# Another set of unread matmuls ahead of the first attention scores

## The chip, the core and the metric

The kernel runs on one core of one Trainium2 chip. Its engines are TensorE (PE; the loading of its weights is listed apart as PEld), VectorE (DVE), ScalarE (ACT), GpSimd (POOL) and SyncE (SP). The metric is the device time of one launch in microseconds, and the time of a kernel is the median of its runs. Profiles come from one execution of the program; its span runs from the first instruction to the last.

## The reference

Sliding-window causal attention (8 batches, 8 heads, 576 positions, head width 64, window 64) feeds a mixer block with a low-rank mix over positions and a two-layer MLP:

```python
scores = scale * q @ k.T                      # kept where 0 <= i - j < 64
attn   = softmax(scores) @ v                  # -> x: 8 x 576 x 512
h      = (x.T @ U) @ V                        # rank 32 over the 576 positions
u      = x + h.T
out    = u + relu(u @ w_ch1) @ w_ch2          # 512 -> 2048 -> 512
```

Inputs and output are float32. The kernel computes with bfloat16 operands and sums in float32.

## The kernel before, in words

Work is ordered by hand: the instructions of each engine stand in its queue in the order in which the Python code calls for them, and an engine takes them strictly in turn, waiting on semaphores for what they read. Loads are issued by POOL (lines 105, 126, 130, 197, 200 and so on).

The program has a prelude for batch 0 and then a loop over nine chunks of 512 rows of the flattened 4608 x 512 activations. A chunk's MLP has 16 column blocks of the first layer (`ch1`, matmuls at line 622, ReLU on ACT at line 633 or DVE at line 631) and then the second layer (`ch2`, line 664). Into the slots between these pieces the attention of the next batch is placed.

The prelude is where the change lies. In PE's queue it has, in this order:

- 91 matmuls called *unread*: `turn_over(91, P)`, line 721, with a 128 x 128 block of the zeroed tile `idle` as weights and 128 columns of the same tile as the moving operand. They write a PSUM tile that nothing reads. They wait only for the memset of `idle` (line 142).
- the scores of batch 0, groups S[0] and S[1] (matmuls at line 311), which need the transposed k and q. These are made on DVE at line 239: k and q of heads 0 to 3 first, then k and q of heads 4 to 7, each after its load.
- two more unread matmuls, of 512 columns: `turn_over(2)`.
- S[2] to S[5], each opened by two matmuls that add a bias (line 287), with the product with v (PV, line 398) between them. Exponentials are on ACT (line 322), masks on DVE (line 329).
- the transposes of the result through PE (line 518), the low-rank mix (lines 444 and 532), ten more unread matmuls of 128 columns, and then chunk 0.

`turn_over` is this helper; each matmul it issues is preceded in PE's queue by a load of its weights:

```python
def turn_over(n, cols=CH, to=None):
    for _ in range(n):
        nc.tensor.matmul(
            (unread if to is None else to)[:, 0, 0:cols],
            idle[:, 0:P],
            idle[:, 0:cols],
            start=to is None,
            stop=to is None,
        )
```

P is 128, W is 64, CH is 512.

Of the kernel before, what the change touches and what calls it, by code (L numbers as in the profile page):

```python
# [16 lines left out]
def kernel(  # L17
# [16 lines left out]
    P = nc.NUM_PARTITIONS  # L34
    W = 64
# [683 lines left out]
# [10 lines that stand above are left out]
    def fresh():  # L729
        return ps_big.tile([P, 2, CH], FP32, name="unread", tag="big")  # L730

    unread = fresh()
    turn_over(91, P)
    att = {0: attention(0, alone=True)}
    a = att[0]
    for f in a["KT"]:
# [125 lines left out]
```

## Time and profile before

| | |
|---|---|
| median of 6 runs | 322.24 us (320.11 to 323.67) |
| the profiled execution's own time | 323.67 us |
| its span | 322.0 us |
| busy in the span: PE / DVE / ACT / POOL | 313.9 / 209.4 / 106.2 / 104.3 us |
| mean granted TensorE clock | 0.979 |
| the 91 unread matmuls | 1.26 to 8.09 us, 219 ns median for one from issue to its modelled end |
| first scores on PE | from 8.29 us |

The busy time of a row counts a matmul from its start to its modelled end, and matmuls overlap; how often one starts is read from counts over a stretch. An idle time in brackets is followed by what ended it. The profile was taken in one execution, and the runs differ among themselves, so a sum is made against 323.67 and 322.0, and only then related to the median. In tables of stretches each engine has its busy time and, in brackets, the number of its instructions that touch the stretch; then come the clock, the share of the DMA engines and GB/s.

### The profile page before, as it was taken

How to read it: one execution, taken by the hardware profiler on the slowest of the kernel's cores; microseconds unless marked ns; L12 is line 12 of the kernel's file. 1: busy time of each engine (PE TensorE's matmuls, PEld its weight loads, DVE VectorE, ACT ScalarE, POOL GpSimd, SP SyncE). 2: the span in 40 equal slices, each digit the busy share in tenths (PEclk: the TensorE clock that was granted, in tenths of full speed). 3: DMA queues.
4: the chain of work that ended last, by engine and by line, in shares of the span. 5: the costliest groups of instructions: out<-in, count | busy, mean ns of one | idle time of the engine just before them, and what ended most of it. 6: DMA issues, size and time to landing. Idle time of an engine off the chain costs nothing.

```text
span 322.0 us, 7022 instructions
## 1 busy us (share of the span) xinstructions
PE 313.9 (97%) x2893; PEld 154.0 (48%) x2893; DVE 209.4 (65%) x368; ACT 106.2 (33%) x174; POOL 104.3 (32%) x156
## 2 busy tenths in 40 slices
PE   8799999999999999999999999999999999999995
PEld 8454454555444544454445444444444444444444
DVE  7543868679698759777957795769577722412211
ACT  1444353274206520552056203630273004203400
POOL 8681429430039403750384037502000200030000
PEclk9759999999999999999999999999999999999999
DMA  7999999999749994899999929993500150050011
GB/s 122 160 199 207 207 157 163 160 204 126 22 114 178 168 105 95 152 168 136 110 180 186 108 52 181 194 139 29 172 2 2 34 164 0 0 163 35 2 65 67
DMA packets 108930, 38.05 MB, mean 118 GB/s; under 512 B 98353, under 2 KB 101809, under 8 KB 108897
## 3 DMA queue, kind: packets, MB, share of 16 engines
q0 software_dynamic: 92480, 25.63, 111.4%
q1 hardware_dynamic: 11232, 10.69, 9.9%
q10 hardware_dynamic: 5184, 1.28, 1.8%
q8 instruction: 23, 0.38, 0.5%
q14 instruction: 11, 0.08, 0.1%
HBM read 48.94 MB, written 9.44 MB: 181 GB/s over the span
## 4 chain that ended last, share of the span: by engine, by line
PE 77%; DMA 12%; DVE 5%; POOL 2%; issue 2%; SPq 1%; ACT 1%; DVEq 0%; POOLq 0%
PE psA L622 32%; PE psU L664 31%; DMA qr<-in_q_dram 7%; DMA vA<-in_v_dram 4%; PE xr L398 3%; PE sc L361 3%; PE psv L473 2%; DVE un L484 1%; DVE stg L560 1%; PE psU L646 1%; SPq L586 1%; POOL kr L114 1%; PE sc L311 1%; PE xT L532 1%; PE xT L518 1%
## 5 line engine op out<-in xcount | busy, mean ns | idle before, releaser
L622 PE MATMUL psA<-uTc,w1b 128*128 128x512 bf16 x576 | 132.9, 380 | 0.0
L664 PE MATMUL psU<-w2b,c 128*128 128x512 bf16 x560 | 127.2, 379 | 0.0
L633 ACT ACTIVATE c<-psA 128x512 bf16<-128x512 f32 x101 | 60.3, 597 | 170.1 <-PE psA L622 170.1
L664 PEld LDWEIGHTS <-c 128*128 128x128 bf16 x560 | 53.5, 98 | 64.5 <-issue 1.9
L622 PEld LDWEIGHTS <-w1b 128*128 128x128 bf16 x576 | 53.4, 98 | 61.3 <-issue 0.2
L586 POOL DMA_DIRECT2D uTc<-stg x35 | 19.1, 556 | 117.1 <-DVE stg L560 77.8
L673 DVE TENSOR_TENSOR osb<-psU,un 128x512 f32<-128x512 f32 x35 | 23.5, 670 | 32.3 <-PE psU L664 32.2
L631 DVE TENSOR_SCALAR c<-psA 128x512 bf16<-128x512 f32 x43 | 29.5, 687 | 22.1 <-PE psA L622 20.5
L126 POOL DMA_DIRECT2D vA<-in_v_dram x32 | 28.2, 886 | 28.2 <-PE psA L622 9.9
L376 DVE TENSOR_TENSOR pts<-pts,mask 128x768 bf16<-128x768 bf16 x42 | 23.0, 556 | 19.8 <-ACT pts L369 17.4
L369 ACT ACTIVATE pts<-sc 128x768 bf16<-128x768 f32 x42 | 31.7, 811 | 3.7 <-PE sc L361 3.7
L484 DVE TENSOR_TENSOR un<-psv,xs 128x512 bf16<-128x512 f32 (+1 forms) x40 | 25.9, 674 | 9.8 <-PE psv L473 9.6
L417 DVE TENSOR_TENSOR xs<-xr,rcp 128x512 bf16<-128x512 f32 (+1 forms) x39 | 26.9, 691 | 1.3
L560 DVE STREAM_TRANSPOSE stg<-un 128x512 bf16<-128x512 bf16 x28 | 18.4, 683 | 0.0
L398 PEld LDWEIGHTS <-pts 128*64 128x64 bf16 x576 | 13.2, 116 | 10.7 <-DVE xs L417 4.7
L247 DVE STREAM_TRANSPOSE qt<-qr 128x576 bf16<-128x576 bf16 x20 | 15.8, 788 | 3.0 <-DMA vA<-in_v_dram 3.0
L114 POOL DMA_DIRECT2D qr<-in_q_dram x20 | 17.0, 851 | 2.1 <-DMA vA<-in_v_dram 1.8
L114 POOL DMA_DIRECT2D kr<-in_k_dram x20 | 16.9, 844 | 2.3 <-DMA vA<-in_v_dram 1.3
L247 DVE STREAM_TRANSPOSE kt<-kr 128x576 bf16<-128x576 bf16 x20 | 15.7, 787 | 1.9 <-DMA kr<-in_k_dram 1.9
L398 PE MATMUL xr<-vB,pts 128*64 128x65 bf16 x320 | 16.2, 202 | 0.6 <-PE xr L398 0.6
L361 PEld LDWEIGHTS <-kt 64*64 64x64 bf16 (+1 forms) x720 | 10.1, 106 | 9.3 <-issue 8.3
L361 PE MATMUL sc<-qt,kt 64*64 64x128 bf16 (+4 forms) x720 | 13.1, 215 | 0.2 <-DVE qt L239 0.2
(70 smaller groups left out, 165.7 us busy)
## 6 DMA issues: line engine op xcount, KB each, us to landing
out_dram<-osb SPq DMA_DIRECT2D x35, 256.0 KB, 2.3
kr<-in_k_dram POOLq DMA_DIRECT2D x26, 288.0 KB, 10.5
qr<-in_q_dram POOLq DMA_DIRECT2D x26, 288.0 KB, 12.1
vA<-in_v_dram POOLq DMA_DIRECT2D x32, 128.0 KB, 13.6
w2b<-in_moe_w_ch_dram POOLq DMA_DIRECT2D x2, 1024.0 KB, 18.3
uTc<-stg SPq DMA_DIRECT2D x42, 32.0 KB, 2.4
uTc<-stg ACTq DMA_DIRECT2D x35, 32.0 KB, 2.3
uTc<-stg POOLq DMA_DIRECT2D x35, 32.0 KB, 2.1
```

The lines of the kernel that those rows point to most:

```text
L114: nc.gpsimd.dma_start(out=dst[32 * part : 32 * (part + 1), off : off + NJJ * RD].rearrange("p (n x) -> p n x", x=r * D), in_=src[b, m * NJ ...
L126: nc.gpsimd.dma_start(out=va[:, t, :, 0:D], in_=v[b, :, t * P : (t + 1) * P, :].rearrange("h p d -> p h d"),)
L247: nc.vector.transpose(out=dst[:, n * S : (n + 1) * S].rearrange("q (m p e) -> q m e p", p=32, e=r), in_=src[:, 32 + n * RD : 32 + (n + 1) ...
L361: nc.tensor.matmul(sc[half * W : (half + 1) * W, g, (a - lo) * W : (z - lo) * W], operand("k", g, jj, e, kb * W, (kb + 1) * W), operand("q ...
L369: nc.scalar.activation(out=dst, in_=sc[:, :, 0 : PB * W].rearrange("p g (n w) -> p g n w", w=W), func=ACT.Exp, scale=scale,)
L398: nc.tensor.matmul(xr[r0 : r0 + W, h // 4, (h % 4) * VW : (h % 4 + 1) * VW], pts[:, g, jj * NB + blk, :], rhs, start=True, stop=True,)
L417: nc.vector.tensor_tensor(out=x[lo:hi, t, :, :].rearrange("p (a h) d -> p a h d", a=2), in0=xv[:, :, :, 0:D], in1=rcp[lo:hi].to_broadcast( ...
L484: nc.vector.tensor_tensor(out=u_tiles[g][rs, :], in0=ps[rs, n, :], in1=xt[n][rs], op=ALU.add)
L622: nc.tensor.matmul(to if c < 2 else to.rearrange("p (t i q) -> p t i q", i=4, t=TPC), w1b[:, dc, n * P : (n + 1) * P], uT_cols(dc), start= ...
L631: nc.vector.tensor_relu(out=c1[i][:], in_=ps)
L633: nc.scalar.activation(out=c1[i][:], in_=ps, func=ACT.Relu)
L664: nc.tensor.matmul(acc[t][:], c1[i][:, t * P : (t + 1) * P], w2b[:, i, :], start=(i == 0), stop=(i == NFC - 1),)
```

## The change

One call becomes two. The 91 matmuls of 128 columns give way to 70 of 64 columns, followed by 30 of 232 columns: 100 matmuls in place of 91, with 11,440 columns in place of 11,648. The weights of each are the same 128 x 128 block as before, loaded anew each time. The PSUM tile, its place in the pool and everything after it are unchanged, and no other engine's queue is touched.

```diff
     unread = fresh()
-    turn_over(91, P)
+    turn_over(70, W)
+    turn_over(30, 232)
     att = {0: attention(0, alone=True)}
```

## The prediction

> **What bounds the kernel now.** I read four views, from the whole to the place of the change. First the page's slices: TensorE (PE) is busy in nine tenths or more of nearly every fortieth of the span, so time taken out of PE's path shows in the end, and time put beside it doesn't.
>
> ```profile
> PE   8799999999999999999999999999999999999995
> PEclk9759999999999999999999999999999999999999
> ```
>
> The reader is to see that only the first three digits, some 24 us, fall short, both in work and in granted clock. The change lies in the first of them. Second, the order of time there:
>
> ```profile
> 1.26 6.83 PE L721 MATMUL unread<-idle 128*128 128x128 bf16 x91 [1.26 <-DVE idle L142]
> ...
> 5.90 1.25 DVE L239 STREAM_TRANSPOSE kt<-kr 128x576 uint32<-128x576 uint32 x1
> 7.00 1.24 DVE L239 STREAM_TRANSPOSE qt<-qr 128x576 uint32<-128x576 uint32 x1
> ...
> 8.29 0.76 PE L311 MATMUL sc<-qt,kt 32*64 32x128 bf16 x48 [0.19 <-DVE qt L239]
> ...
> 8.97 0.61 PE L721 MATMUL unread<-idle 128*128 128x512 bf16 x2
> ...
> 9.42 0.49 PE L287 MATMUL sc<-bias,ident 128*128 128x384 bf16 x2
> ...
> 10.15 1.26 DVE L239 STREAM_TRANSPOSE qt<-qr 128x576 uint32<-128x576 uint32 x1 [0.21 <-DMA qr<-in_q_dram]
> ...
> 11.47 0.85 PE L311 MATMUL sc<-qt,kt 32*64 32x128 bf16 x24 [1.56 <-DVE qt L239]
> ```
>
> The 91 unread matmuls end at 8.09. The first scores start at 8.29, and what lets them go is not PE but the transpose of q, which ends at 8.24. Later PE stands still again, for 1.56 us up to 11.47, for the second q transpose, and that one waits for its load. Third, the chain of waits says the same of what sets the end:
>
> ```profile
> 3.08 7.05 DMA qr<-in_q_dram
> 10.13 0.02 issue
> 10.15 1.27 DVE qt L239
> 11.42 0.04 issue
> 11.47 0.85 PE sc L311 x19
> ```
>
> No L721 of the first group stands in the chain: it runs from the q load through the transpose to the scores at 11.47, and from there mostly on PE. Fourth, the stretches, cut where the matmuls' rate or the granted clock changes:
>
> ```profile
> 1.26:4.60 3.34, 3.34 (x32) 3.34 (x33) 2.20 (x14) 0.84 (x1) 3.07 (x8) 1.00 0.57 89
> 4.60:8.03 3.43, 3.43 (x62) 3.33 (x60) 3.16 (x6) 0.00 (x0) 3.43 (x5) 1.00 1.11 200
> 8.03:11.43 3.40, 1.69 (x54) 1.15 (x53) 2.74 (x4) 1.51 (x2) 2.98 (x5) 1.00 1.97 166
> 11.43:14.84 3.41, 3.37 (x68) 1.78 (x71) 1.90 (x6) 1.62 (x2) 1.74 (x3) 0.50 2.22 145
> 14.84:18.26 3.42, 3.42 (x108) 2.49 (x102) 1.44 (x4) 1.52 (x2) 2.68 (x5) 0.50 1.45 191
> 21.67:25.08 3.41, 3.41 (x19) 2.06 (x19) 0.00 (x0) 0.96 (x2) 1.03 (x2) 0.50 1.14 213
> ```
>
> In brackets first stands the number of matmuls. 32 unread ones fit in the first stretch and 62 in the second of nearly equal length: 107 ns each, then 56 ns. So PE starts slow and is released at about 4.60 (the clock column reads 1.00 there although the rate says half; it is full only from 4.60). In 8.03:11.43 PE is busy for only 1.69 of 3.40 us, and from 11.43 to 25.08 the clock is 0.50. These 13.65 us at half clock, in which PE is nearly all of the chain, are the costly thing that the warm-up could touch.
>
> **The change, part by part.** *Removed:* 91 matmuls of 128 columns. 31 at 107 ns and 60 at 56 ns are 3.32 + 3.36 = 6.68 us, plus the last one's own tail, which gives the 6.83 of the row. *Added, seventy of 64 columns:* no row has 128-wide weights with 64 columns. From 128 columns in 107 ns slow, 64 take 53 ns if the columns set the pace. Until the release, 3.34 us after the start, 3.34 / 0.053 = 63 of them are done; the other 7 run at half of 56, 28 ns: 0.20 us. *Added, thirty of 232 columns:* 232/128 of 56 ns is 101 ns, thirty are 3.04 us. Sum: 3.34 + 0.20 + 3.04 = 6.58 against 6.68, so 0.1 us earlier: 11,440 columns in place of 11,648, and nine more instruction pairs that the columns cover. The last unread matmul ends at about 7.99. The cover is the transpose until 8.24: of the gain nothing is seen, and if the cover were gone it would be worth the 0.1 us.
>
> Is the pace of the short ones really set by columns? Each of them loads 128-wide weights anew. The row to go by is the attention product at half clock, whose weights also change every time:
>
> ```profile
> 17.42 1.40 PEld L398 LDWEIGHTS <-pts 128*64 128x64 bf16 x48
> ```
>
> 48 loads in 1.40 us, 29 ns for a load with its matmul of 65 columns, two of which (upper and lower half) go together. So a pair of instructions needs no more than 29 ns to issue, less than 53. The load itself: the Trainium skill, page "TensorE: Matmul & The Clock Gate", section "LDWEIGHTS (loading the stationary operand)", has a rule that speaks against the change: a load takes its number of columns over 1.2 ns, 107 ns for 128. By it the short ones would be bound by their loads: 31 until the release, 39 more at no less than 56 ns, 2.18 us, and the sum would be 3.34 + 2.18 + 3.04 = 8.56, PE free at 9.8. The rows are against it: the 62 matmuls of 4.60:8.03 each carry a 128-wide load and come every 56 ns, and a load over 128 columns (98 ns mean at full clock, L622) shows no longer than one over 64 (L361, 106). I take 53 ns, and keep 107 as the other end. Even then the 1.56 us of idle ahead of 11.47 plus the 0.19 ahead of 8.29 take up the delay of 1.7 us.
>
> What is queued behind on PE: the first two score groups, two unread matmuls of 512 columns, the first biases; for them wait the exponentials on ScalarE (8.87) and the masks on VectorE (11.26, behind the transposes until 11.41). A delay of up to about a microsecond is lost in that queue. DMA queues, SP, POOL, ScalarE and VectorE issue exactly what they did, in the same order.
>
> *The release itself.* Nothing in the rows shows how short matmuls count in whatever grants the clock. The same page, section "What's actually happening", says that the warm-up is some 3.4 us of time and not a number of matmuls; the trace's first release after 3.34 us agrees, and by that rule the release stays at 4.60: cost 0. But the stretch 14.84:18.26 is 3.42 of 3.42 us busy, mostly with matmuls of 64 and 65 columns, and the clock stays at 0.50 after it; 21.67:25.08, with 128 and 512 columns, is followed by full clock. The narrow weights there (32 rows, 64 columns) are one reading, the shortness another. So the other end: the seventy short ones don't count, 70 x 53 ns = 3.73 us are lost for the release, and only the thirty longer ones can earn it. Between these ends I take 0, because the short ones here use all 128 rows and columns.
>
> The span stays 322.0 and the profiled execution 323.67 (1.67 outside the span). That execution lies 1.43 above the median of 322.24; the edit touches nothing that makes this gap, so the forecast is carried over to the median: 322.2 us.
>
> **The rivals.** *Slower:* the short ones don't count, and the thirty don't earn the release in time. They run slow, 232/128 x 107 = 194 ns each: 3.73 + 5.82 = 9.55, PE free at 10.8. The two score groups at half clock (0.78 each, as from 11.47 to the biases), two unread of 512 at 427 ns and the biases (0.75) are 3.2 us: the scores of 11.47 start at 14.0 at the latest, about 2.3 us late with some overlap, and from there PE is the chain: 324.5. It decides once PE is free later than about 9.85. For it: the stretch of short matmuls that earned no clock. Against: there the array was partly used.
>
> *Faster:* PE is late but not too late (free at 9.5 to 9.9, by a release one stretch later, at 8.03, or by load-bound short ones). Then 8.03:11.43 has little idle time left, and the clock may not be taken at 11.43. One stretch of 3.41 us at full instead of half clock is worth up to 1.7 us: 320.5; two, with the exponentials (0.81 each) and value copies as new limits, perhaps 3: 319.2. For it: the clock fell right after the one stretch with PE half idle. Against: it needs the warm-up to be slower than its columns say, and the scores themselves, 32 rows deep, may not hold the clock.
>
> *No change because it isn't longer:* "nine more" is 2% fewer columns; that is the forecast itself.
>
> **How the numbers follow.** About 0.5% (1.6 us) is what a measurement of this kernel can tell from no change; the six runs alone go from 320.11 to 323.67. Forecast 0.47, with its own range 321.0 to 323.4; slower rival 0.31; faster rival 0.22. The range over the cases is 319.9 to 325.0: from between the two faster ends to a little past the slower one.
>
> **What would show it.** Right: seventy unread matmuls 53 ns apart until about 4.6 and thirty 100 ns apart, ending near 8.0; first scores still released by the q transpose; scores at 11.47 as before; half clock again for about four such stretches. The load rule is right if the short ones come 107 ns apart. The slower rival shows as thirty matmuls 194 ns apart and scores after 11.47 that wait for PE; the faster one as a clock above 0.50 between 11.4 and 14.8. The prediction is wrong above all if the release moves, or if the grid of these stretches lies elsewhere from one execution to the next and the two forms meet it differently.

## The result: 0.5% slower

The changed kernel takes 323.3 us in the median (30 runs) against 321.68 us of the kernel before (67 runs). The ratio is 1.0049, with a 95% interval of 1.0032 to 1.0065. The prediction was no change, 322.2 us. Executions more than 1.5% slower than the fastest of their kernel are left out of every ratio, mean and count.

The order of time of the changed kernel (start, length, engine, line, operation):

```profile
1.26 6.78 PE L721 MATMUL unread<-idle 128*128 128x64 bf16 x100 [1.26 <-DVE idle L142]
...
8.39 0.76 PE L311 MATMUL sc<-qt,kt 32*64 32x128 bf16 x48 [0.35 <-DVE qt L239]
...
12.13 1.25 DVE L239 STREAM_TRANSPOSE qt<-qr 128x576 uint32<-128x576 uint32 x1 [1.77 <-DMA qr<-in_q_dram]
12.65 0.54 POOL L206 DMA_DIRECT2D ub<-in_moe_U_dram  x1 [2.19 <-DMA qr<-in_q_dram]
13.44 0.85 PE L311 MATMUL sc<-qt,kt 32*64 32x128 bf16 x24 [3.43 <-DVE qt L239]
```

The first row merges both new sizes (100 matmuls). It ends at 8.04, a little earlier than before, and the first scores again wait for a transpose. The scores that stood at 11.47 now start at 13.44, and PE has idled for 3.43 us before them. The transpose of q is not to blame: it waited 1.77 us for its load. So did POOL, by 2.19 us, with the loads that it still had to issue. The chain of waits names the same load:

```profile
3.07 9.04 DMA qr<-in_q_dram
12.11 0.02 issue
12.13 1.27 DVE qt L239
13.40 0.04 issue
13.44 0.85 PE sc L311 x16
```

Before, this load stood there with 7.05 us and ended at 10.13. By the semaphore of the load, 15 of its 16 pieces had landed by 10.48 and the last one landed at 12.11; before, they landed by 9.78 and at 10.13. Two stretches of the DMA queues show what shared the way with it. From 8.5 to 10.1 us the changed kernel has this row; the kernel before has no row of that queue there, and has it from 10.1 to 11.2 (the second fence; the columns are packets, MB and share of 16 engines):

```profile
q8 instruction: 1, 0.02, 3.7%
```

```profile
q8 instruction: 1, 0.02, 5.4%
```

It is one packet of 16 KB, and it takes 0.94 us. That the queue brings PE's instructions is read from its count over the whole kernel: 23 packets here, 22 in a form below that has 90 PE instructions fewer. The packet starts at 9.86 us in the changed kernel, ahead of the last piece of q, and at 10.22 us before, just behind it (10.13). In this profile the last piece is 1.63 us behind the fifteenth, more than the packet's 0.94; what makes up the rest isn't shown. Last, the stretches of the changed kernel:

```profile
1.26:4.80 3.54, 3.54 (x67) 3.54 (x68) 2.24 (x15) 0.84 (x1) 3.28 (x9) 1.00 0.60 90
4.80:8.00 3.20, 3.20 (x38) 2.98 (x35) 3.10 (x6) 0.00 (x0) 3.20 (x4) 1.00 1.07 192
8.00:11.63 3.63, 1.66 (x53) 1.12 (x53) 1.59 (x2) 1.51 (x2) 2.46 (x4) 1.00 1.89 167
11.63:25.28 13.65, 11.10 (x212) 7.20 (x212) 7.05 (x17) 5.57 (x13) 9.40 (x14) 0.50 1.48 172
```

The release at 4.80 comes with 67 short matmuls in 3.54 us, 53 ns each. The half-clock time is 13.65 us again, in both profiled executions. One profile thus shows the late load. It can't show how often the clock falls. For that I counted stretches over all executions, since each run lists the mean granted clock.

### The profile page after: what moved, and what is told of

Its sections match the earlier page's. It is cut to its first block, busy times and chain, and to the rows that moved or that the text cites. A ratio compares the mean times of both kernels' runs of the same rounds, so it can differ in the third digit from the quotient of the medians.

```text
span 322.4 us, 7040 instructions
## 1 busy us (share of the span) xinstructions
PE 312.8 (97%) x2902; PEld 153.9 (48%) x2902; DVE 209.6 (65%) x368; ACT 106.2 (33%) x174; POOL 104.3 (32%) x156
## 4 chain that ended last, share of the span: by engine, by line
PE 64%; DMA 20%; DVE 6%; SPq 3%; issue 3%; POOL 3%; ACT 1%; POOLq 0%; DVEq 0%
PE psA L622 27%; PE psU L664 24%; DMA qr<-in_q_dram 10%; DMA vA<-in_v_dram 7%; SPq L586 3%; PE xr L398 3%; PE sc L361 2%; DMA uTc<-stg 2%; DMA kr<-in_k_dram 2%; PE psv L473 2%; POOL kr L114 1%; DVE stg L560 1%; PE psU L646 1%; PE sc L311 1%; DVE un L484 1%
## 5 line engine op out<-in xcount | busy, mean ns | idle before, releaser
L361 PE MATMUL sc<-qt,kt 64*64 64x128 bf16 (+3 forms) x720 | 13.1, 215 | 0.2 <-DVE qt L239 0.2
```

The lines of the kernel that those rows point to most:

```text
L361: nc.tensor.matmul(sc[half * W : (half + 1) * W, g, (a - lo) * W : (z - lo) * W], operand("k", g, jj, e, kb * W, (kb + 1) * W), operand("q ...
```

## The experiments

All forms were timed against the kernel before on the same chip, but for a third profile of the changed kernel, which is one execution. Only the prelude is edited. "Stretches" are half-clock stretches of 3.41 us: each takes 3.41 x 0.5 / 322 = 0.0053 off an execution's mean granted clock, so they can be counted from it. In 179 executions of the kernel before, 0, 1, 2, 3 and 4 stretches came 36, 44, 36, 27 and 36 times (1.91 on the mean), with medians of 320.98, 321.21, 321.48, 322.29 and 323.07 us. A line through these executions rises by 0.54 us for each stretch. The kernel before differs from set to set: beside the forms of the first theory it had 2.31 stretches on the mean, beside the later ones 1.63 to 1.75. In 31 executions of the changed kernel the counts were 0, 0, 4, 9 and 18.

The summary first. "144th" is when PE starts the 144th instruction of its queue (loads of weights and matmuls counted), "fetch" is the start of the first 16 KB packet of instructions, "q" is when the last piece of the second q load lands, all in us from one profile; stretches are means over the timed executions.

| kernel | 144th | fetch | q | stretches | ratio (95%) |
|---|---|---|---|---|---|
| before | 6.82 | 10.22 | 10.13 | 1.91 | 1 |
| changed: 70 x 64, 30 x 232 | 5.00 | 9.86 | 12.11 | 3.45 | 1.0049 (1.0032 to 1.0065) |
| the same again | 5.16 | 8.87 | 11.04 | 3.46 | 1.0056 (1.0033 to 1.0078) |
| the same, a third profile | 5.16 | 8.79 | 10.97 | | |
| 182 x 64 | 5.04 | 8.85 | 11.03 | 3.50 | 1.0067 (1.0027 to 1.0108) |
| 100 x 116 | 7.70 | 11.53 | 10.14 | 2.71 | 1.0004 (0.9981 to 1.0027) |
| 55 x 64, 36 x 225 | 6.48 | 10.23 | 10.05 | 1.67 | 0.9982 (0.9961 to 1.0004) |
| 46 x 254 | 9.14 | 12.75 | 10.19 | 2.29 | 0.9987 (0.9960 to 1.0014) |
| 109 x 107 | 6.98 | 11.39 | 10.12 | 1.58 | 1.0027 (1.0001 to 1.0053) |
| 30 x 232, 70 x 64 | 8.32 | 12.16 | 9.82 | 2.41 | 1.0017 (0.9996 to 1.0037) |
| before, q transposed late | 6.58 | 10.12 | 10.04 | 3.43 | 1.0050 (1.0027 to 1.0073) |
| before, filled | 7.78 | 11.50 | 10.02 | 0.76 | 0.9974 (0.9953 to 0.9995) |
| changed, filled | 5.16 | 8.85 | 11.03 | 0.64 | 1.0038 (1.0014 to 1.0061) |
| filled, q transposed late | 6.73 | 10.65 | 9.91 | 0.50 | 0.9997 (0.9976 to 1.0017) |

### First theory: more instructions bring the fetch forward

My first theory was that eighteen more instructions put the fetch in front of q. Its rival was that the short matmuls shift the clock's release. Four forms of the warm-up with nearly the same number of columns separate number and size.

```diff
-    turn_over(91, P)
+    turn_over(100, 116)
```

> 100 unread matmuls of 116 columns: as many instructions as the changed kernel, 11,600 columns, no short ones. Fetch theory (the block of PE's instructions, 16 KB, is fetched at 9.86 us instead of 10.22, because 18 more instructions stand ahead of it, and holds up the last piece of the second q load): slower than before like the changed kernel, ratio 1.004 to 1.006, the fetch at 9.6 to 10.0, q landed at about 12. Rival (the short matmuls shift the clock's release and the scores): they are gone, ratio 1.000.

```diff
-    turn_over(91, P)
+    turn_over(55, W)
+    turn_over(36, 225)
```

> 55 unread matmuls of 64 columns and 36 of 225: as many instructions as before, 11,620 columns, short ones first as in the changed kernel. Fetch theory: the fetch is at about 10.2 again and q lands near 10.1, ratio 0.998 to 1.002. Rival (short ones): most of the change is still there, ratio 1.004 to 1.005.

```diff
-    turn_over(91, P)
+    turn_over(46, 254)
```

> 46 unread matmuls of 254 columns: 90 PE instructions fewer than before, 11,684 columns. Fetch theory: PE comes to the fetching place only with the scores after 11.47, the fetch starts later than 12 us, q and the first three v loads land undisturbed, ratio 0.995 to 1.000. Rival (short ones): no short ones, as before, ratio 1.000; it gives no reason for a gain.

```diff
-    turn_over(91, P)
+    turn_over(109, 107)
```

> 109 unread matmuls of 107 columns: 36 PE instructions more than before, 11,663 columns. Fetch theory: the fetch comes a little earlier still, at 9.4 to 9.8, and holds up q just as much, ratio 1.004 to 1.008. Rival (short ones): no short ones, ratio 1.000.

The first theory, as I had put it, fell. With 100 even matmuls the fetch came at 11.53, later and not earlier, q landed at 10.14 and the ratio was 1.0004. With 109 the fetch came at 11.39. Its core held up, though: in all four the fetch came after q and q landed in time, so none lost anything there. The mixed form, with short ones in front but 55 instead of 70, was as fast as before. So shortness alone isn't the cause either. The form of 46 showed that a far later fetch (12.75) gains nothing that can be measured. The ratio of the 109 form is not explained by anything here: q is in time and the stretches are few. Its one profile shows PE standing still for 3.68 us far from the edit, and a half-clock stretch from 187.15 on:

```profile
187.02 0.52 PE L473 MATMUL psv<-hh,vrep 128*128 128x512 bf16 x1 [3.68 <-DVE un L484]
```

VectorE had waited 3.55 and 1.53 us for loads there, ahead of its transposes of k and q (line 247). Whether other executions do the same, and why, stays open.

### Is it the edit, and is it the order?

```diff
-    turn_over(91, P)
+    turn_over(70, W)
+    turn_over(30, 232)
```

> The changed kernel itself once more, on one chip with the others. Each half-clock stretch of 3.41 us that an execution has takes 0.0053 off its mean granted clock; in 58 executions of before, 0 to 4 stretches came 6, 14, 11, 10 and 17 times, in 31 of the changed kernel 0, 0, 4, 9 and 18 times. Clock theory (the edit itself makes the long half-clock time the usual one): again no execution with 0 or 1 and most with 3 or 4, ratio 1.003 to 1.006. Chance theory ([...]not the edit): 0 and 1 come up in a third of them, ratio 1.000. Fetch theory (later landing of q): ratio 1.005 and q late at about 12 us again.

```diff
-    turn_over(91, P)
+    turn_over(182, W)
```

> 182 unread matmuls of 64 columns, 11,648 columns as before: all short. Clock theory in the form that short ones earn the release sooner: release not later than 4.8 us in the profile, nearly all executions with 3 or 4 stretches, ratio 1.004 to 1.008. In the form that it is the long ones after the short that matter: as before, ratio 1.000. Chance theory: ratio 1.000. Fetch theory: the block is fetched much earlier, before 9 us, q late, ratio 1.004 or more.

```diff
-    turn_over(91, P)
+    turn_over(30, 232)
+    turn_over(70, W)
```

> The thirty of 232 columns first, then the seventy of 64: the same matmuls and columns as the changed kernel in the other order. Clock theory in the form that short ones earn the release sooner: the long ones are at the front now, stretches spread from 0 to 4 as before, ratio 0.998 to 1.001. Chance theory: the same, ratio 1.000. Fetch theory (number of instructions): slower like the changed kernel, ratio 1.004 to 1.006.

The changed kernel repeated itself: 1.0056, with 0, 0, 0, 7 and 6 executions of 0 to 4 stretches. Chance as the explanation is out. Its release came at 7.14 in this profile, far later than 4.80, and q was late all the same. Its chain of waits and its row of scores:

```profile
3.07 7.97 DMA qr<-in_q_dram
...
11.06 1.27 DVE qt L239
...
12.37 0.54 PE sc L311 x22
```

All-short lost too. Here PE itself also stood still, in the middle of its first scores (order of time of this kernel; "issue" is a wait for nothing that the profile shows):

```profile
8.42 0.70 PE L311 MATMUL sc<-qt,kt 32*64 32x128 bf16 x41
11.40 0.27 PE L311 MATMUL sc<-qt,kt 32*64 32x128 bf16 x7 [2.28 <-issue]
```

The packet was under way from 8.85 to 9.80 us and PE went on at 11.40. That it waited for instructions is likely, but not shown.

The swapped order has the same hundred matmuls as the changed kernel, the same instructions and columns. Its fetch came at 12.16, q landed at 9.82, and two thirds of the loss were gone (1.0017, an interval that holds 1), between what the two theories had expected. What is left, 0.50 us in the means, is nearly what its 0.78 stretches more than before timed beside it cost (x 0.54 = 0.42); why it has more isn't shown. So neither the number of instructions nor the sizes alone decide. What fits is how early PE has got through a certain number of instructions: the fetch starts 3.4 to 3.9 us after the 144th in twelve of the fourteen profiles, 4.4 and 4.9 in the other two (the changed kernel's first profile is the 4.9). Any count from about 130 to 147 fits as well. Seventy short matmuls in front are 140 instructions, done at about 5.0 us; in the forms that don't start so, PE gets there at 6.5 to 9.1. The five profiles whose fetch started before 10 us are those whose q landed at 10.97 to 12.11; in the nine others it landed between 9.82 and 10.19.

In each of the five it is one piece of sixteen that is late. In four of them fifteen have landed by 10.03 to 10.30 and the last comes 0.73 to 1.00 us later, about the length of the packet (1.63 in the first profile); in the nine others the last is at most 0.35 us behind the fifteenth.

### Second theory: a late q, and what it does to the clock

If this is right, a late transposed q alone must bring the loss, without any change to PE's queue. A memset on VectorE delays its transpose:

```diff
-    for f in a["KT"]:
+    scratch = const.tile([P, 1024], FP32, name="scratch")
+    for n, f in enumerate(a["KT"]):
+        if n == 3:
+            nc.vector.memset(scratch[:], 0.0)
         f()
```

> The kernel before with one memset of about 1.07 us on VectorE between the third and the fourth transpose, so that the second q transpose starts near 11.0 instead of 10.15; PE's queue is untouched. Late-q theory (the short matmuls at the front bring PE sooner to its 144th instruction, about which the next block of instructions is asked for; the fetch then runs into the second q load, which lands 0.9 to 2 us late, PE idles longer and the half-clock stretches get more): scores of 11.47 start near 12.3, 0 and 1 stretches become rare, ratio 1.002 to 1.005. Clock theory (only how the unread matmuls are counted): the late scores are made up for later, stretches as before, ratio 1.000 to 1.001.

The order of time of this kernel:

```profile
9.98 0.91 DVE L739 MEMSET scratch<- 128x1024 f32 x1
...
10.81 1.20 DVE L239 STREAM_TRANSPOSE qt<-qr 128x576 uint32<-128x576 uint32 x1
12.06 0.53 PE L311 MATMUL sc<-qt,kt 32*64 32x128 bf16 x24 [2.02 <-DVE qt L239]
```

The scores came 0.59 us later than at 11.47. The ratio was 1.0050, and the stretches went to 3.43: the same loss and the same clock as in the changed kernel, from VectorE alone. So a late q does both. The time is lost once as lateness, and once more because PE, idle for longer, has its clock halved more often or for longer. The sum closes: 1.68 stretches more than before timed beside it (1.75) x 0.54 us are 0.91 us, with the 0.59 us of lateness 1.50 us, and the means differ by 1.50 us. The tile `scratch` isn't the cause, since the last form below has it too and loses nothing.

The traces also show what goes before a fall of the clock. From the release on it changes only at steps of 3.41 us. Of the full-clock stretches in the preludes of the fourteen profiles (PE's busy time counted in each, narrow matmuls like wide ones), five had PE busy for 1.14 to 1.77 us, and half clock followed each of them; none of those with more than 2.5 us was followed by it. Between 1.9 and 2.5 us both occur. In the three profiles of the changed kernel the stretch with the late scores had 1.62 to 1.77 us.

The other way round, the idle time can be filled. Five unread matmuls of 512 columns in place of two stand ahead of the scores of 11.47:

```diff
-    turn_over(91, P)
+    turn_over(88, 132)
 ...
-    turn_over(2)
+    turn_over(5)
```

> 88 unread matmuls of 132 columns, and five of 512 in place of two after the first two score groups: PE's idle time ahead of 11.47 is 0.65 us shorter, the number of PE instructions is that of before. Late-q theory: the fetch stays where it was (10.2 to 11.6), q lands at about 10.1, and fewer executions fall to half clock at 11.4: ratio 0.996 to 1.000. Clock theory: 0.996 to 1.000 as well; if only the scores' own low use of the array decides, 1.000 to 1.002.

```profile
9.54 1.25 PE L721 MATMUL unread<-idle 128*128 128x512 bf16 x5
10.63 0.49 PE L287 MATMUL sc<-bias,ident 128*128 128x384 bf16 x2
11.36 0.53 PE L311 MATMUL sc<-qt,kt 32*64 32x128 bf16 x24 [0.23 <-DVE qt L239]
```

Here 0.23 us of idle time are left. The stretches fell to 0.76, and 10 of 21 executions had none. The ratio is 0.9974: this form is faster than both kernels. Fewer stretches account for it: 1.0 fewer than in the executions of before timed beside it (1.75) x 0.54 us is 0.53 us, against a difference of means of 0.66 us.

A longer filling in the changed kernel:

```diff
     turn_over(70, W)
     turn_over(30, 232)
 ...
-    turn_over(2)
+    turn_over(8)
```

> The changed kernel with eight instead of two unread matmuls of 512 columns after the first two score groups (1.3 us more on PE at full clock, into the idle time ahead of the late scores). Late-q theory: q is still late (11 to 12), the idle time is gone; what is left of the loss is the lateness alone, ratio 1.001 to 1.004, with a stretch fewer on the mean. If the idle time has no part in it: 1.005 as in the changed kernel.

A third profile, of the changed kernel as it is:

> The changed kernel, a third look. Late-q theory: PE's 144th instruction at 5.0 to 5.2, the fetch between 8.8 and 9.9, the last piece of the second q load at 11 or later, against 10.1 to 10.2 where the fetch comes after it. If the two earlier looks were chance, the fetch lies after 10.1 and q lands at about 10.1.

And the filled form with the late q:

```diff
-    turn_over(91, P)
+    turn_over(88, 132)
 ...
+        if n == 3:
+            nc.vector.memset(scratch[:], 0.0)
 ...
-    turn_over(2)
+    turn_over(5)
```

> The filled form (88 unread matmuls of 132 columns, then five of 512) with the memset of the late-q form on VectorE: q's second transpose some 0.6 to 0.9 us late, the clock's loss mostly filled away. If lateness and half-clock stretches simply add (0.53 us for each stretch in the executions of before), stretches lie between those of the filled form (0.76 on the mean) and of the late-q form (3.43), and the ratio between 0.9974 and 1.005: 1.000 to 1.003. If a late q costs more than its lateness even with the clock kept, as the changed kernel with the filling seems to show: 1.003 to 1.006 with fewer than two stretches on the mean.

In the last of these the sum closes once more:

```profile
11.95 0.53 PE L311 MATMUL sc<-qt,kt 32*64 32x128 bf16 x24 [1.38 <-DVE qt L239]
```

Its scores started at 11.95, 0.48 us late, with 0.50 stretches against 1.74 of before timed beside it (0.76 to 3.43 were expected). Lateness and clock, added, give 0.48 - 1.24 x 0.54 = -0.19 us; measured in the means were 321.38 - 321.59 = -0.21 us. The third profile of the changed kernel had the early fetch and the late q again.

The changed kernel with the filling doesn't fit so well: its clock was kept (0.64 stretches), and yet it took 1.0038. Its scores start at 12.36, 0.9 us late, and the missing stretches should have paid for 0.6 of them; more than a microsecond is left over. Its one profile shows 1.41 us of it in the loop, at the same matmul as in the form of 109:

```profile
185.89 0.39 PE L473 MATMUL psv<-hh,vrep 128*128 128x512 bf16 x1 [1.41 <-DVE un L484]
```

Again VectorE had waited for loads ahead of these transposes (1.22 and 1.58 us). The filled form of before has no such wait there. That this is what the other executions lose, and that the edit brings it about, is not shown. A second fetch, or the later loads that POOL issues behind q, were not tried apart.

## Why the prediction was wrong

*The work and its pace: right.* In the first profile the short matmuls came 53 ns apart, 67 of them, the three after the release 29 ns, the long ones 99 ns; predicted were 63 at 53, seven at 28 and the long ones at 101. The last one ended at 8.04 instead of 7.99. The load rule of 107 ns was rightly set aside.

*The cover by the first q transpose: right where the release is early.* It was at 4.80 in the first profile, and the first scores waited for the transpose. In the second it was at 7.14, about eleven of the long ones ran slow, 193 ns apart, and the scores started at 9.10; PE still idled for 1.65 us before the later scores, so they weren't held up by that. Releases from 4.11 to 7.23 us stand in the profiles; the form with the latest (100 x 116) was as fast as before. So the release "at 4.60" of the prediction was the place in one execution: the changed kernel alone has it at 4.80, 7.14 and 6.71. That the first profile came so near was luck. The prediction's last sign of being wrong, that these stretches lie elsewhere from one execution to the next, is what the runs show.

*The slower rival: right sign, wrong mechanism.* It had 324.5 us, 2.3 more; measured were 1.6 more in the medians. The short ones do earn the release (67 of them, nothing else, by 4.80; in the all-short form by 5.16), and the late scores wait for q, not for PE.

*The faster rival: a right step, but not in this kernel, and a wrong size.* Less idle time ahead of the scores does keep the clock, as the filled form shows. One stretch was put at up to 1.7 us; 1.0 stretch fewer brought 0.66 us there, and the line through the executions gives 0.54.

*The step that failed* is the sentence "DMA queues, SP, POOL, ScalarE and VectorE issue exactly what they did, in the same order". The order is unchanged for all that the program issues. It left out the one queue that PE itself drives: the page of before has it as "q8 instruction", 23 packets with 0.38 MB. I gave that row no thought, at half a percent of the engines. With the short matmuls in front PE is through its 144th instruction at 5.0 to 5.2 instead of 6.8, the fetch starts 0.4 to 1.4 us earlier, the packet of 0.94 us falls ahead of the last piece of the load that leads the chain, and q lands 0.8 to 2.0 us later. So the term "scores at 11.47 as before", put at nothing, was 1.97, 0.90 and 0.83 us in the three profiles. The Trainium skill, page "Runtime: NRT & Kernel Launch", section "Instruction fetch mechanics", says that each engine's sequencer fetches its instructions in blocks of 16 KiB over its own DMA queue, and that the cost of crossing a block is mostly hidden. The packet size agrees with the traces. For PE itself the changed kernel's profiles don't contradict "hidden": it waits for q there. But the load beside the packet isn't spared, it lands 0.8 to 2.0 us later, and in the all-short form PE stood for 2.28 us, perhaps for instructions.

*The sum.* Means over the executions of before and of the changed kernel (179 and 44) are 321.86 and 323.22 us: 1.36 us. Stretches went from 1.91 to 3.45: 1.54 x 0.54 = 0.83 us, and 0.5 us is left. The second measurement alone, with before timed beside it, gives 1.83 x 0.54 = 0.99 of 1.30 us, and 0.3 us is left. The scores are 0.8 to 2.0 us late, so lateness and clock, added, are too much for the changed kernel: some of the lateness is made good later. How much of it, in general, isn't known. The two first profiles show it in one case: the difference is 1.97 us at the second scores and 1.16 us at the loop's first matmul, because the four matmuls of line 532 come after the release in the changed kernel (0.88 us on the chain, 1.71 before); it is 0.42 us at the end, mostly because PE in the profile of before stands for 0.28 and 0.37 us at 186.84 and 220.35 and in the other doesn't.

Shown are the late landing of one piece with the early fetch, in all five profiles that have it and in none of the nine others, and the loss through a late q by itself. That the packet is what holds up the piece is argued from their times and lengths, and that the request is tied to a fixed place in PE's instructions from the fit of the times; no run moved the fetch or that place alone.

## What to carry to other kernels

A warm-up has a cost in instructions as well as in time: in this kernel PE, with 140 short instructions in front, had its next block fetched up to 1.4 us sooner, and the packet fell beside the load that the start of the kernel waits for. Before a reordering that is "hidden", look up where the rows of the instruction queue fall beside the load that leads the chain, and keep the packet behind it. And where the clock falls after idle time, count how often over many executions: one profile shows one state of it.

## What the runs showed that was not expected

The clock of one and the same kernel differs from execution to execution: from none to four half-clock stretches of 3.41 us, 0.54 us of time for each, which accounts for about half of the variance of the time. In twelve of the thirteen profiles that have any, all of them lie in the prelude; the mean clock alone doesn't tell where. An idle time of PE about half a microsecond longer moved nearly all executions to three or four stretches, three more unread matmuls of 512 columns moved most of them to none or one.
